# Two exp tiles of a pair turned by VectorE and moved in one set of larger transfers, with new engine orders

## Chip, cores and metric

One core of a Trainium2 chip runs the whole program in one launch. The metric is the device time of one execution in microseconds. Names used here: PE is TensorE's matmul, PEld its weight load, DVE is VectorE, ACT is ScalarE, POOL is GpSimd, SP is SyncE, whose queue issues most DMA transfers (SPq). PSUM is the memory into which PE writes.

## The reference

Attention over 2 x 8 heads (sequence 1152, width 64, queries averaged in pairs to 576), then two dense blocks on the 1152 tokens of width 512:

```python
def _attn_ref(q, k, v):
    q_pool = q.reshape(B, H, S // 2, 2, D).mean(axis=3)
    scores = scale * np.matmul(q_pool, k.transpose(0, 1, 3, 2))
    scores = scores - np.max(scores, axis=-1, keepdims=True)
    attn = np.exp(scores)
    attn = attn / (np.sum(attn, axis=-1, keepdims=True) + 1e-09)
    return np.matmul(attn, v)

def _moe_ref(x, w_in, w_out):
    h = x @ w_in
    g = np.maximum(h, 0.0) + np.log1p(np.exp(-np.abs(h)))
    return g @ w_out

def _moe2_ref(x, w_gate, w_val, w_out, rms_g):
    rms = np.sqrt(np.mean(x * x, axis=-1, keepdims=True) + 1e-06)
    xn = x / rms * rms_g
    return (silu(xn @ w_gate) * (xn @ w_val)) @ w_out
```

All inputs are float32, and the kernel keeps their precision by splitting operands into a rounded high part and a low rest (three products in place of one).

## The kernel before

The attention goes over 8 pairs of heads (`NP`, index `pb`), and in each pair over tiles `x` of 128 queries: four for each head (`NF`, tiles 0 to 3) and one mixed tile of 64 queries of both heads (`x == NF`, tile 4). One step of a tile is: scores on PE into PSUM (`qk`, L700), the row maximum on DVE (`softmax`, L714), the exps on ACT (L716) into a buffer `p`. The product with v (`av`, L778) needs the exps with keys on the partitions, so each 128x128 piece has to be turned. In most tiles PE turns them: `flip` (L735) makes 18 transposes a tile (9 blocks of keys, two heads) in five groups into PSUM, and ACT or DVE copies each group out into the buffer `pt` (`copy`, L357 and L359), five copies a tile. `flip_m` (L1188) does it for the mixed tile.

Tiles in `STREAMED`, tile 1 of pairs 1 to 6, go another way: `stream` turns the exps in blocks of 32x32 with two DVE transposes (L756, one for each head) into a buffer `turned`, and 16 DMA transfers on SP (L761) carry the blocks to their partitions in `moved`, from which `av` reads in place of `pt`. A transfer carries 32 partitions of 576 columns, 72 KB.

`prep` loads q, k and v of the next pair (L368) and makes their parts: `kk` (k with its low rest, on POOL or DVE, L362) and `qh`, `ql` (L675, L677, L617). `scales` and `shift` divide by the sums. During the attention the weights of the first dense block are decoded beside it (`decode`, called through `first_pair` and `first_out`): the weights arrive as pairs of words, L427 on ACT, L432 and L438 on DVE put them together, then a rounding copy (ACT) and a subtraction (POOL or DVE) make the halves. In the "exp" form this is done in two cuts of 512 columns; in the "soft" form, used after the attention, in one of 1024, with one more DVE operation (L435) and the subtraction on DVE. Two blocks of `w1`, and two of `w1o` (`first_out`, called in pairs 6 and 7), are decoded in the attention.

Behind it stand the two dense blocks, long runs of products (`product`, L893; `expand`, L959 to L961; `alone_in`, L980; `main_out`, L1394). The first expansion with the second block of `w1o` reads its halves at its own place in PE's order.

What sets the order of the work is a list written out in the kernel, `ORDER`: one word for each of 2314 operations, a letter for the engine (p PE, v DVE, a ACT, g POOL, s SP) and the operation's number in the source. Each engine runs its words in that order; waits between engines follow from the buffers. The marker word n1 stands where the attention's buffers are given back. `AREAS` are the columns of the memory areas, from which `alloc` cuts buffers; a buffer cut from a place used before waits for all work on the earlier one. At the start `heat` runs transposes of the identity (L1226), 20 ahead of the first scores and 16 behind the first two.

Of the kernel before, what the change touches and what calls it, by code (L numbers as in the profile page):

```python
# [37 lines left out]
AREAS = {"KF": 11264, "KR": 18432, "MR": 8704, "LR": 12800, "LF": 5120}  # L38
# [3 lines left out]
EARLY = 6.0  # L42
WAIT = 4.5
# [3 lines left out]
STREAMED = {(pb, 1) for pb in range(1, NP - 1)}  # L47
# [7 lines left out]
    p53 v7 s10 q11 v3 v8 s13 q12 a52 v6 v2 v4 v5 s14 v9 s15 v23 s16 v24 v25 s17 a35 v26 v27 s18 v36 a28 a30 v29 s19 a39 v31 a37 v40 p54 s20 v32 v38 a33 v34 s21  # L55
    v55 p57 s22 p60 v41 a56 v58 s63 a42 p91 p96 s62 v43 a92 v46 a59 p93 v47 v44 v94 a97 p98 a99 p100 v48 a95 p105 v101 p102 v45 v106 g69 p107 v103 p112 g68 a108
    p109 g70 a51 v113 s65 p114 v110 a104 s61 v71 v72 p116 a115 a111 p118 v117 p120 v119 s66 a49 p123 a86 v121 p125 a124 p127 a126 s64 v50 p130 v128 p132 a131
    a122 v87 v82 v83 p134 a133 v78 a129 p136 v135 g77 p138 g79 v137 g85 a73 s221 p141 p143 v142 p145 v139 g84 a144 s222 a88 g74 a140 p148 v146 p150 g76 v149
    a147 g75 p152 v151 a80 v89 p154 v90 a153 p158 v81 s220 a155 p156 v159 g228 p161 a157 a162 p163 g229 p165 v164 g227 a160 s224 p168 v166 p170 a245 a230 s225
    v169 a167 v201 v231 s173 p192 v246 p194 v171 a232 v193 p197 v195 g235 p199 a198 s67 g236 a196 p211 v200 g237 s172 p213 v212 g234 p215 v214 a241 g238 p218  # L60
    v216 p268 a219 g243 s223 a239 p271 v269 a217 g242 s348 v250 a270 s226 p273 g244 a272 p276 s347 v274 p278 a277 g233 p281 a275 v279 v251 a282 p283 a280 p285
    p287 v284 s266 a286 v202 s255 p290 a247 s260 p292 v288 p294 a293 s203 a291 s263 v248 a289 v240 p297 s267 p299 v295 g354 s253 a298 g353 s262 v355 s257 a296
    s258 p301 v300 v371 p303 s256 v175 a174 p307 v302 s207 a304 s259 v249 p305 p310 a306 s204 v372 a311 v308 p312 s261 p314 a313 s205 a356 s265 p317 p319 a318
    v330 s206 a309 v315 s254 s252 v357 s350 p321 a320 v176 a316 p323 v322 s351 p326 v324 a184 p328 a327 s264 s346 p337 a329 a325 p339 v338 p341 v178 g210 a340
    p344 g363 v342 p394 a345 g209 p397 g208 v395 a343 g364 v376 a396 p399 v367 a398 p402 v400 g362 p404 a403 g369 s502 p407 v405 a401 g368 p409 s503 v408 a406
    p418 v410 s349 v373 p420 a419 v331 p422 a421 v377 s332 a358 p425 p427 p429 v423 a428 s388 g361 a426 s385 g360 s380 p432 v430 a424 p434 s381 g359 s378 v433
    a431 s382 v365 s391 g370 p436 v435 a375 s336 p438 v437 p442 s392 v374 v366 a439 s334 p440 a414 s386 p445 g508 v441 g185 v443 a446 p447 s335 p449 a448 s333
    a177 s384 g509 p452 v450 p454 a453 s390 a444 s387 v510 s389 v485 a451 v415 s393 p476 s379 v179 p478 a455 s383 v477 g180 a186 p481 s352 v479 p483 a482 s501
    v181 a480 p492 v182 p496 v484 g413 v493 g187 a188 p494 v497 p499 a495 p549 s505 g412 a500 a498 g183 p552 v550 s506 g411 v532 a551 p554 v531 a553 a190 p557
    p562 a558 p559 v555 g191 a522 p564 v563 g189 a556 v560 p569 v486 a565 s543 a561 p573 s535 v526 v513 s487 p571 a570 p580 v527 v574 g516 s544 a511 s504 a572  # L70
    g524 p576 v581 p578 a577 s537 a579 p583 s536 a575 p585 v514 s507 v512 v584 a582 g517 s542 g515 p587 v586 s533 p589 a588 v523 s491 a590 v518 p591 s489 v519
    a592 p596 v528 s633 v520 p593 a597 v521 a530 v525 p598 s541 p603 v594 p600 s634 a599 a416 p605 v601 s488 a595 g417 s548 s490 v604 v616 a602 s545 v529 p607
    v640 s538 p609 v608 g639 a606 s540 g641 p612 v610 s546 p614 a613 s547 a642 s539 p623 a657 v615 a611 s534 v643 p627 s632 v624 p625 v658 v628 p630 a626 p680
    a631 g567 p683 v681 a629 g566 s637 g568 a682 s636 v662 p685 s456 a644 v684 p688 v686 p690 a689 g646 p693 v691 a687 p695 s457 g649 g648 v694 a692 g650 v663
    p702 s635 a696 a703 p704 v617 p706 a705 s665 a653 g645 s669 p709 v707 p711 s677 p713 a651 g654 s674 v712 a710 s618 a659 g655 a708 p716 v714 s671 p718 g647
# [91 lines left out]
class Plan:  # L167
# [36 lines left out]
    def around(self, tag, cols, bufs, areas, end=0):  # L204

        bases = [self.alloc(cols, areas, end) for _ in range(bufs)]
# [105 lines left out]
def body(ctx: ExitStack, tc: tile.TileContext, kT, qT, v, w1, w1o, wg, wv, w2o, rg, outM, outR):  # L312
# [651 lines left out]
    def tile_ring():  # L964
        return rings["g"]()
# [626 lines left out]
```

## Time and profile before

| what | value |
|---|---|
| time, median of 3 runs | 653.26 us (651.52 to 653.35) |
| the profiled execution: its time | 651.38 us |
| the profiled execution: its span, first to last instruction | 649.6 us |
| PE busy | 639.1 us, 98% of the span |
| DVE busy | 489.5 us, 75% |
| ACT busy | 393.4 us, 61% |
| POOL busy | 154.1 us, 24% |
| transposes of the flips (L735) | 468 |
| DVE transposes (L756) | 12 |
| transfers `turned` to `moved` (L761) | 96 |

The busy shares are averages over the span. The attention takes about the first 236 us, the dense blocks the rest. The chain of waits follows the work that ended last back from the last instruction; in a window it shows which engine's work set the time there.

### The profile page before, as it was taken

To read this page: it belongs to the slowest core of one execution; us is meant where nothing else is said; L and a number is where in the kernel's file an instruction comes from. 1 tells how busy PE (TensorE), PEld (TensorE's weight loads), DVE (VectorE), ACT (ScalarE), POOL (GpSimd) and SP (SyncE) were. 2 spreads that over 40 slices of the span, in tenths; PEclk is the share of its full clock that TensorE was granted. 3 is DMA by queue.
4 is the path that set the end of the run, shared out by engine and by line. 5 is a ranking of instruction groups with operands and counts; after the bars stand their busy time and mean duration, and the time that the engine had idled before them with its cause. 6 is when DMAs were issued, how large, how long until landed. Compare 5 with 4: busy or idle time off the path is not lost.

```text
span 649.6 us, 11166 instructions
## 1 busy us (share of the span) xinstructions
PE 639.1 (98%) x4376; PEld 545.6 (84%) x4376; DVE 489.5 (75%) x717; ACT 393.4 (61%) x647; POOL 154.1 (24%) x156
## 2 busy tenths in 40 slices
PE   7999999999999999999999999999999999999997
PEld 6888999898889988888888888888888888888886
DVE  8889889888898878887787477659898778766210
ACT  5777788788878876555553584355455544553221
POOL 0442435344523531020210033201010020104010
PEclk9999999999999999999999999999999999999999
DMA  6454544667474540332301110300542231310002
GB/s 182 125 179 104 145 102 122 155 188 189 101 202 106 159 144 1 125 135 98 126 37 66 65 66 2 129 1 0 195 147 80 99 129 66 131 65 1 34 32 81
DMA packets 25026, 66.78 MB, mean 103 GB/s; under 512 B 5327, under 2 KB 6286, under 8 KB 24974
## 3 DMA queue, kind: packets, MB, share of 16 engines
q1 hardware_dynamic: 24462, 65.68, 33.0%
q8 instruction: 34, 0.56, 0.4%
q10 hardware_dynamic: 512, 0.40, 0.2%
q14 instruction: 18, 0.15, 0.1%
HBM read 56.59 MB, written 2.39 MB: 91 GB/s over the span
## 4 chain that ended last, share of the span: by engine, by line
PE 95%; DVE 2%; ACT 1%; issue 1%; DMA 1%; ACTq 0%; DVEq 0%
PE s L893 25%; PE t L778 12%; PE s L700 12%; PE s L1394 9%; PE t L735 8%; PE t L893 4%; PE s L961 3%; PE s L959 3%; PE s L960 3%; PE t L1394 3%; PE t L980 2%; PE s L980 2%; PE t L1006 2%; PE s L1006 1%; PE t L1188 1%; PE t L961 1%
## 5 line engine op out<-in xcount | busy, mean ns | idle before, releaser
L714 DVE TENSOR_REDUCE nm<-s 128x1 f32<-128x1152 f32 x72 | 97.1, 1352 | 15.1 <-PE s L700 13.9
L716 ACT ACTIVATE p<-s,nm 128x1152 f32<-128x1152 f32 x72 | 88.1, 1225 | 14.4 <-DVE nm L714 13.6
L735 PE MATMUL t<-ident,p 128*128 128x128 f32 x468 | 69.0, 278 | 2.4 <-ACT p L716 1.3
L357 ACT COPY pt<-t 128x512 f32<-128x512 f32 (+2 forms) x105 | 54.2, 534 | 27.6 <-PE t L735 20.9
L778 PE MATMUL t<-pt,v 128*64 128x128 f32 (+1 forms) x1224 | 66.8, 263 | 0.0
L778 PEld LDWEIGHTS t<-pt,v 128*64 128x64 f32 x1224 | 59.6, 137 | 6.7 <-issue 4.5
L357 ACT CAST areaKR<-areaKF 128x1024 fp32r<-128x1024 f32 (+1 forms) x52 | 46.5, 896 | 29.6 <-PE t L1394 14.7
L735 PEld LDWEIGHTS t<-ident,p 128*128 128x128 f32 x468 | 53.0, 141 | 12.5 <-issue 3.4
L362 POOL TENSOR_TENSOR areaLR<-areaLF,areaLR 128x512 fp32r<-128x512 f32 x11 | 17.7, 1610 | 148.1 <-ACT areaLR L357 110.6
L362 DVE TENSOR_TENSOR areaKR<-areaKF,areaKR 128x1024 fp32r<-128x1024 f32 (+1 forms) x36 | 39.2, 1093 | 15.7 <-ACT areaKR L357 15.6
L893 PE MATMUL s<-areaMR,areaKR 128*128 128x512 f32 x192 | 49.0, 395 | 0.0
L362 DVE TENSOR_TENSOR areaKF<-areaKF 128x256 f32<-128x256 f32 (+1 forms) x91 | 48.0, 552 | 0.6
L893 PE MATMUL s<-areaKR 128*128 128x512 f32 x180 | 46.7, 397 | 0.0
L438 DVE SCALAR_TENSOR_TENSOR areaKF<-areaKF 128x1024 int32<-128x1024 int32 (+1 forms) x38 | 45.7, 1206 | 0.9 <-ACT areaKF L427 0.2
L357 ACT CAST areaLR<-areaKF 128x1024 fp32r<-128x1024 f32 (+1 forms) x33 | 29.2, 890 | 24.3 <-DVE areaKF L362 12.8
L362 POOL TENSOR_TENSOR kk<-kr,kk 64x384 fp32r<-64x384 f32 x35 | 34.7, 1007 | 34.3 <-ACT kk L357 26.0
L893 PEld LDWEIGHTS s<-areaMR,areaKR 128*128 128x128 f32 x192 | 35.3, 188 | 7.6
L427 ACT ACTIVATE areaKF<-areaKF 128x1024 f32<-128x1024 f32 (+1 forms) x38 | 39.9, 1054 | 1.2 <-DMA areaKF<-in_w1o_dram 1.0
L893 PEld LDWEIGHTS s<-areaKR 128*128 128x128 f32 x180 | 32.9, 188 | 6.9
L893 PE MATMUL s<-areaKR,areaLR 128*128 128x512 f32 x144 | 37.1, 396 | 0.0
L362 POOL TENSOR_TENSOR qs<-qr 128x224 f32<-128x224 f32 (+1 forms) x35 | 20.9, 617 | 66.3 <-DVE qm L636 21.2
L359 DVE COPY pt<-t 128x512 f32<-128x512 f32 (+2 forms) x49 | 30.0, 621 | 6.8 <-PE t L735 3.3
(274 smaller groups left out, 1465.7 us busy)
## 6 DMA issues: line engine op xcount, KB each, us to landing
areaKF<-in_w_dram SPq DMA_DIRECT2D x16, 512.0 KB, 5.1
areaKF<-in_w1o_dram SPq DMA_DIRECT2D x16, 512.0 KB, 4.7
qr<-in_qT_dram SPq DMA_DIRECT2D x28, 288.0 KB, 4.8
areaKF<-areaKF SPq DMA_DIRECT2D x96, 72.0 KB, 2.2
areaKF<-in_wg_dram SPq DMA_DIRECT2D x12, 512.0 KB, 4.5
areaKF<-in_wv_dram SPq DMA_DIRECT2D x12, 512.0 KB, 4.6
areaKF<-in_w2o_dram SPq DMA_DIRECT2D x12, 512.0 KB, 4.4
v<-in_v_dram SPq DMA_DIRECT2D x16, 288.0 KB, 3.4
```

The lines of the kernel that those rows point to most:

```text
L357: nc.scalar.copy(out, in_)
L359: engines[e].tensor_copy(out, in_)
L362: engines[e].tensor_tensor(out=out, in0=in0, in1=in1, op=o)
L427: o = op([act(n)], lambda e, x0=x0, x1=x1: nc.scalar.activation(out=word(1, x0, x1).bitcast(F32), in_=word(1, x0, x1).bitcast(F32), scale= ...
L438: op([dve(n)], lambda e, x0=x0, x1=x1: nc.vector.scalar_tensor_tensor(out=word(1, x0, x1), in0=word(1, x0, x1), scalar=3, in1=word(0, x0, ...
L700: nc.tensor.matmul(sc()[:, c, :N], lhsT=q()[:, cut], rhs=k()[:, c * N:(c + 1) * N], start=(i == 0), stop=(i == len(todo) - 1))
L714: u["mx"] = op([dve(S, psum=True)], lambda e: nc.vector.tensor_reduce(out=nm(), in_=sc()[:, :, :N], axis=AX.XY, op=ALU.max, negate=True), ...
L716: o = op([("ACT", 1.42)], lambda e: nc.scalar.activation(out=pr(), in_=sc()[:, :, :N], func=AF.Exp, bias=nm(), accum_out=s["den"]()[:, col ...
L735: nc.tensor.transpose(t()[:, i * P:(i + 1) * P], pr[:, c * P:(c + 1) * P], ident)
L778: nc.tensor.matmul(t()[h * D:h * D + D, :n], lhsT=s["v"][h]()[:, c, :], rhs=rhs, start=(c == 0), stop=(c == CK - 1))
L893: nc.tensor.matmul(bank(), lhsT=a(k), rhs=b(k), start=start and k + i == 0, stop=stop and k + i == 3, skip_group_check=seeded)
L1394: nc.tensor.matmul(out[m](), lhsT=w, rhs=g(), start=j + i == 0, stop=last and j == js[-1] and i == 2)
```

## The change

Tile 3 of pairs 1 to 5 is turned in the same way as tile 1 (`STREAMS`, `DOUBLE`). The two tiles of a pair share one `turned` and one `moved` of twice the size. The four DVE transposes write their parts of `turned`; the 16 transfers start when all four are done, and each carries 1152 columns, 144 KB. The products of both tiles with v run in the next pair, in the source at its tiles 2 and 3 (`WHEN`). Pair 6 still turns tile 1 alone.

The two buffers `pt` of 2304 columns become a fixed `ptwhole`, a `ptmixed` of half the size, and places inside `moved` and two later cuts (`spare`, `turned`). The areas are cut anew. The second `first_out` no longer runs in pair 7 but after the attention, in the "soft" form, in a place that the last pair's tile 3 uses until its product is done. `load` and the other transfers have new latencies in the figures with which the order was made; the kernel's run does not read them.

`ORDER` is new throughout. It has 2270 words in place of 2314. Counted in the two lists:

| words | PE | DVE | ACT | POOL | SP |
|---|---|---|---|---|---|
| before, all | 601 | 713 | 574 | 150 | 268 |
| after, all | 576 | 701 | 567 | 150 | 268 |
| before, ahead of n1 | 277 | 303 | 276 | 110 | 205 |
| after, ahead of n1 | 250 | 290 | 266 | 100 | 203 |

At the start the 16 warming transposes stand ahead of the first scores (`p53 p60 p54 p57` in place of `p53 p54 p57 p60`).

```diff
-AREAS = {"KF": 11264, "KR": 18432, "MR": 8704, "LR": 12800, "LF": 5120}
+AREAS = {"KF": 15872, "KR": 14336, "MR": 8704, "LR": 16896, "LF": 864}
+WHEN = {2: (1,), 3: (3,)}
-STREAMED = {(pb, 1) for pb in range(1, NP - 1)}
+END = NP - 2
+DOUBLE = (1, 2, 3, 4, 5)
+STREAMS = {pb: (1, 3) if pb in DOUBLE else (1,) if pb else () for pb in range(NP)} | {NP - 1: ()}
...
+    def use(self, base, first=0, n=0):
+
+        cut = slice(first * 2 * S, (first + n) * 2 * S) if n else slice(None)
+        b = Buf(lambda: base()[:, cut])
+        n = max(n, 1)
+        tail = base.__dict__.setdefault("tail", {})
+        b.area, b.prior = base.area, base.prior + [tail[x] for x in range(first, first + n) if x in tail]
+        tail.update((x, b) for x in range(first, first + n))
+        base.users.append(b)
+        self.placed.append(b)
+        return b
...
+    def place(pb, x):
+        if x == NF:
+            return places["mixed"]
+        return places["whole" if x % 2 == 0 else ("turned" if (pb, x) == (NP - 1, 3) else "spare")]
+
+    def laid_out(t, n):
+        return t().rearrange("p (b x h c j) -> p x h c b j", b=P // G, x=n, h=2, j=G)
+
     def stream(pb, x):
 
-        turned, moved = rings["turned"](), rings["moved"]()
-        units[pb, x, 0]["pt"] = moved
+        s, n = st[pb], len(STREAMS[pb])
+        i = STREAMS[pb].index(x)
+        if i == 0:
+            s["turned"], s["moved"] = plan.use(places["turned"], 0, n), plan.use(places["moved"], 0, n)
+        turned, moved = s["turned"], s["moved"]
         for h in range(2):
             pr = units[pb, x, h]["p"]
             op([("DVE", 1.37, 1)], lambda e, h=h, pr=pr: nc.vector.transpose(
-                turned().rearrange("p (b h c j) -> p h c b j", b=P // G, h=2, j=G)[:, h],
-                pr().rearrange("p k (c b j) -> p (k c) b j", b=P // G, j=G)), r=[(pr, None)], w=[(turned, h)])
+                laid_out(turned, n)[:, i, h], pr().rearrange("p k (c b j) -> p (k c) b j", b=P // G, j=G)),
+               r=[(pr, None)], w=[(turned, (i, h))])
+        if i < n - 1:
+            return
+        w = n * GW
         for b in range(P // G):
             for a in range(P // G):
                 op([("SP", 0.62)], lambda e, a=a, b=b: nc.sync.dma_start(
-                    out=moved()[b * G:(b + 1) * G, a * GW:(a + 1) * GW], in_=turned()[a * G:(a + 1) * G, b * GW:(b + 1) * GW]),
-                   r=[(turned, 0), (turned, 1)], w=[(moved, (a, b))], lat=4.0)
-
-    def av(pb, x):
+                    out=moved()[b * G:(b + 1) * G, a * w:(a + 1) * w], in_=turned()[a * G:(a + 1) * G, b * w:(b + 1) * w]),
+                   r=[(turned, None)], w=[(moved, (a, b))], lat=2.4)
+
+    def av(pb, x, more=False):
...
-    early = {(1, 0): [(first_pair, 0, HURRY[0])], (3, 0): [(first_pair, 1, HURRY[1])], (6, 0): [(first_out, 0, HURRY[2])],
-             (7, 0): [(first_out, 1, HURRY[3])]}
+    early = {(1, 0): [(first_pair, 0, HURRY[0])], (3, 0): [(first_pair, 1, HURRY[1])], (7, 0): [(first_out, 0, HURRY[2])]}
...
+            if x in STREAMS[pb]:
                 stream(pb, x)
                 qk(pb, x + 1, 0)
-                av(*prev)
-                qk(pb, x + 1, 1)
-                prev = late.pop() if late else None
-                late.append((pb, x))
+                avs(then + before)
+                if x < NF - 1:
+                    qk(pb, x + 1, 1)
+                after()
                 continue
...
     rooms(3)
+    first_out(1, "soft", FS, RS)
     first_out(2, "soft", FS, RS)
     first_pair(2, "soft", FS, RS)
```

## Rows read from the trace of the kernel before

**Rows 1.** The page's first part: busy us, share of the span, instructions.

```profile
PE 639.1 (98%) x4376; PEld 545.6 (84%) x4376; DVE 489.5 (75%) x717; ACT 393.4 (61%) x647; POOL 154.1 (24%) x156
```

**Rows 2.** The chain's shares by line: 30.96 to 231.65, then 170.15 to 199.67 us.

```profile
by line: PE s L700 34.4%; PE t L778 33.8%; PE t L735 22.9%; PE t L1188 3.4%; issue 0.9%; DVE qlB L617 0.8%; DVE kk L362 0.8%; DVE nm L714 0.7%; ACT p L716 0.7%; ACT pt L357 0.6%; DVE pt L359 0.6%; PE t L1191 0.4%; DVE O L359 0.2%; DVEq L359
...
by line: PE t L778 32.7%; PE s L700 30.3%; PE t L735 19.9%; DVE qlB L617 5.8%; DVE kk L362 5.4%; issue 2.8%; DVE pt L359 2.4%; PE t L1188 0.4%; PE t L1191 0.4%
```

**Rows 3.** Windows: length, busy us of PE, PEld, DVE, ACT, POOL, clock, DMA, GB/s.

```profile
30.96:231.65 200.69, 197.38 (x2127) 179.50 (x2126) 172.32 (x229) 163.59 (x287) 84.72 (x99) 1.00 0.55 150
142.40:170.15 27.75, 27.73 (x303) 25.30 (x302) 23.35 (x31) 24.26 (x44) 14.71 (x17) 1.00 0.53 138
170.15:199.67 29.52, 28.09 (x302) 25.40 (x302) 27.07 (x35) 23.84 (x41) 11.93 (x14) 1.00 0.59 156
```

**Rows 4.** The chain in order of time, pair from 57.60: start us, us, what.

```profile
66.45 2.12 PE t L778 x36
68.56 0.59 PE t L735 x4
69.15 1.05 PE s L700 x6
70.20 0.44 PE t L735 x4
```

**Rows 5.** Groups by line, whole span: busy us, mean ns, idle before and releasers.

```profile
L357 ACT COPY pt<-t 128x512 f32<-128x512 f32 (+2 forms) x105 | 54.2, 534 | 27.6 <-PE t L735 20.9 <-PE t L1188 3.1 <-PE t L1191 2.1
...
L359 DVE COPY pt<-t 128x512 f32<-128x512 f32 (+2 forms) x49 | 30.0, 621 | 6.8 <-PE t L735 3.3 <-PE t L1188 2.3 <-PE t L1191 0.9
...
L756 DVE STREAM_TRANSPOSE areaKF<-p 128x1152 f32<-128x1152 f32 x12 | 16.2, 1355 | 0.0
```

**Rows 6.** Transfers of L761: landing; then timeline of SP and PE, one set.

```profile
DMA to landing us min/median/max: 1.9/2.2/4.4
...
110.59 1.18 SPq L761 DMA_DIRECT2D areaKF<-areaKF  x2
...
123.61 4.39 SPq L761 DMA_DIRECT2D areaKF<-areaKF  x7
...
137.39 2.19 PE L778 MATMUL t<-areaKF,v 128*64 128x128 f32 x36
```

**Rows 7.** Timeline of DVE, then POOL, 167 to 179 us: start, us, what, idle.

```profile
167.26 1.36 DVE L756 STREAM_TRANSPOSE areaKF<-p 128x1152 f32<-128x1152 f32 x1
...
171.80 0.62 DVE L617 SCALAR_TENSOR_TENSOR qlA<-qs,qhA 128x512 fp32r<-128x512 f32 x1
...
174.33 0.29 DVE L359 COPY O<-t 128x128 f32<-128x128 f32 x1 [0.22 <-PE t L778]
...
177.96 1.69 DVE L617 SCALAR_TENSOR_TENSOR qlB<-qs,qhB 128x512 fp32r<-128x512 f32 x1
...
167.33 1.99 POOL L362 TENSOR_TENSOR kk<-kr,kk 64x384 fp32r<-64x384 f32 x2 [3.77 <-issue]
...
176.01 3.10 POOL L362 TENSOR_TENSOR areaKR<-areaKF,areaKR 128x512 fp32r<-128x512 f32 x2
```

**Rows 8.** Behind the attention: one window, then timelines of PE and DVE.

```profile
250.00:271.00 21.00, 21.00 (x105) 17.59 (x104) 18.86 (x30) 13.31 (x21) 1.63 (x1) 1.00 0.03 7
...
242.16 3.23 PE L778 MATMUL t<-pt,v 128*64 128x128 f32 x72
...
271.19 0.39 PE L959 MATMUL s<-areaLR,areaMR 128*128 128x512 f32 x1
...
250.03 0.69 DVE L432 TENSOR_SCALAR areaKF<-areaKF 128x1024 int32<-128x1024 int32 x1
...
251.72 1.25 DVE L435 SCALAR_TENSOR_TENSOR areaKF<-areaKF 128x1024 f32<-128x1024 f32 x1
...
255.67 1.22 DVE L438 SCALAR_TENSOR_TENSOR areaKF<-areaKF 128x1024 int32<-128x1024 int32 x1
```

**Rows 9.** Timeline of PE at the start.

```profile
9.90 1.91 PE L1226 MATMUL t<-ident 128*128 128x128 f32 x16
```

More of the change, by code (lines that the diff above doesn't have):

```diff
@@ L42 @@
 EARLY = 6.0
+WHEN = {2: (1,), 3: (3,)}
+SOON = {1: (1,), 2: (3,)}
 WAIT = 4.5
@@ L59 @@
[L59 to L62, printed above, removed]
@@ L204, in around @@
     def around(self, tag, cols, bufs, areas, end=0):
-        bases = [self.alloc(cols, areas, end) for _ in range(bufs)]
+        bases = [self.alloc(cols, a, end) for a in (areas if isinstance(areas, list) else [areas] * bufs)]
         count = [0]
@@ L657, in prep @@
                 round_q(h, ("m0", "m1"), 0, f, slice(0, f))
-                op([dve(S, True), act(S)], lambda e, kk=kk, hi=hi: copy(e, kk()[hi], kr()[hi]),
-                   r=[(kr, None)], w=[(kk, ("h", c)) for c in range(KB)])
+                w = [(kk, ("h", c)) for c in range(KB)]
+                if pb in CASTS:
+                    op([("POOL", 0.6)], lambda e, kk=kk, hi=hi, h=h: nc.gpsimd.dma_start(out=kk()[hi], in_=kT[n + h]),
+                       w=w, lat=6.3, hurry=8.0)
+                else:
+                    op([dve(S, True), act(S)], lambda e, kk=kk, hi=hi: copy(e, kk()[hi], kr()[hi]), r=[(kr, None)], w=w)
                 for c, cut, m in kcuts:
@@ L726, in flip @@
         if "pt" not in first:
-            first["pt"] = ring("a", "pt", [P, CK, 2, P], F32, 2)
+            first["pt"] = plan.use(places["moved"], x // 2, 1) if pb < END and x % 2 else plan.use(place(pb, x))
         pt = first["pt"]
+        laid = lambda: pt().rearrange("p (c h q) -> p c h q", h=2, q=P)
         t = tbank()
@@ L1164, in rooms @@
             free_ring("room")
-        rings["room"] = plan.around(f"room{plan.frees}", 2 * W, n, f"KF:0:{n * 2 * W}")
+        rings["room"] = plan.around(f"room{plan.frees}", 2 * W, n, [f"KF:{i * 2 * W}:{(i + 1) * 2 * W}" for i in range(n)])
     def turn(pb, x):
@@ L1267, in body @@
                 flips[1]()
-                if prev:
-                    av(*prev)
-                    if prev in STREAMED:
-                        shift(pb - 1)
-                if pb and x == 0:
-                    scales(pb - 1)
-                    if (pb - 1, 1) not in STREAMED:
-                        shift(pb - 1)
-                flips[2]()
-                if x == 1 and late:
-                    av(*late.pop())
-                    if last:
-                        free_ring("turned", "moved")
-                    shift(pb - 1)
+                avs(then + before)
+                after()
+                flips[2]()
                 flips[3]()
@@ L1441, in body @@
     norm_flip(nb)
-    late = [plan.alloc(T, "LF KF", -1) for _ in range(3)]
+    late = [plan.alloc(T, "KF LF", -1) for _ in range(3)]
     steps = {J: seven((("wg", J), ("wv", J)), X2, *banks, m2_done(J, late[1] if J == 2 else None),
```

256 lines of the change are left out of this document (144 added, 112 removed).

## The prediction

> **What bounds the kernel now.** I read the page first. PE is busy 639.1 of 649.6 us [rows 1]. Its granted clock is 1.00 in every window, so a change of clock level plays no part [rows 3, 8]. An engine that is always busy need not always be the limit, so the chain of waits comes next, window by window. In the attention, from 31 to 232 us, the chain is PE for 34.4 + 33.8 + 22.9 + 3.4 + 0.4 = 94.9%; the other 5.1% of 200.7 us, 10.2 us, is time in which PE waited for DVE or ACT [rows 2]. Those waits are not spread evenly: in the pair from 142.40 PE is busy 27.73 of 27.75 us, in the pair from 170.15 the chain is 16.4% something else, 4.8 of 29.52 us [rows 2, 3]. Behind the attention (250 to 271 us stands for it) PE is busy 21.00 of 21.00 [rows 8]. So the reader should see two stages: a long product stage where only PE work counts, and an attention stage where PE work counts plus some 10 us of waits. The engine next to the limit in the attention is DVE, 172.3 of 200.7 us (86%), with ACT at 163.6 (82%) [rows 3].
>
> **Removed from PE.** Five tiles (tile 3 of pairs 1 to 5) lose 18 transposes each. Four take 0.44 us where nothing disturbs them, 0.11 each, and 0.59 where they follow the product with v [rows 4]. Five times 18 times 0.11 is 9.9 us. One 0.59 instead of 0.44 per tile goes too: 0.15 x 5 = 0.75 us (between 0 and 1.5). The products with v themselves stay: 2.12 us for 36 matmuls on evicted tiles, and the same spacing on moved ones, whose runs of 32 columns stay as they are [rows 4, 6]. PE is the chain wherever these transposes stand, so this is worth **10.65 us**, if nothing else becomes late.
>
> **Moved between DVE and ACT.** The same five tiles lose 25 evictions out of PSUM: 0.53 us on ACT or 0.62 on DVE as means [rows 5]. They gain ten DVE transposes of 1.355 us, 13.6 us [rows 5]. The decode of the second block of `w1o` leaves the attention: there it costs DVE two shifts and two or-operations of half the width of those in [rows 8]; I estimate them at half of 0.69 and of 1.22, 1.9 us in all. The order written in the kernel tells the rest: ahead of the marker n1 DVE has 13 instructions fewer and ACT 10 fewer. Ten were added and four went with the decode, so 19 other DVE instructions go. Each costs between 0.29 (a copy 128 wide) and 0.62 us, 5.5 to 11.8 us [rows 5, 7]. DVE thus changes by 13.6 - 1.9 less 5.5 to 11.8, between -0.1 and +6.2; I take +2, nearer to the lower end, because most of the copies that can move are the wide ones. ACT falls by about 10 x 0.53 = 5.3 us. Together they have 335.9 + 2 - 5.3 = 332.6 us in some 2 x 191, 87%; before it is 335.9 in 2 x 200.7, 84% [rows 3]. The pair without a wait ran at (23.35 + 24.26) / 55.5 = 86%, the worst one at 86.2% too [rows 3]: load alone does not decide the waits up to here, but 87% lies just past what was seen. I add **+1.5 us** to the 10.2 us of waits. Its ends are -8 (a new order could be free of them, as the wait-free pair is) and +8.
>
> A rule speaks against this part. Here the PE way costs 18 x 0.11 = 1.98 us of PE and five evictions a tile; the DVE way costs 2.71 us of DVE, the engine that is next to the limit, and transfers on top [rows 4, 5]. The Trainium skill's page "VectorE: DVE Perf Modes", section "Rules for kernel authors", says to transpose a full 128x128 on TensorE when its PSUM destination is acceptable, and to keep DVE for blocks of 32x32. By the engine-time that the rule compares, the change would lose 2.71 - 1.98 = 0.73 us a tile, 3.7 us in all; by the chain it gains 10.65, since PE's time ends last. The case in which the rule wins is the first rival below.
>
> **Transfers.** The count stays at 96, 16 for each of six pairs, but those of pairs 1 to 5 carry 144 KB instead of 72. A transfer of 72 KB lands after 1.9 to 4.4 us, median 2.2 [rows 6]. For twice the bytes I bound it by the same 2.2 and by twice that, 4.4, and take 2.6, since a landing this much longer than a single issue is mostly not bytes. SP issues two in 1.18 us, 16 in 9.4 us; interleaved with loads the set now takes from 110.59 to 128.00, 17.4 us, and the product that reads it begins at 137.39, 9.4 us later [rows 6]. After the change the set cannot start before the transposes of tile 3. By PE sums (scores twice 1.05, flips 1.98, product 2.12 a tile [rows 4]) these end about 20 us into a pair of 25.6 us; 17.4 us later is 12 us into the next pair, and its tile 2, where the first reader stands in the source, runs from about 9.5 to 15.7. The cover is thus 0 to 4 us instead of 9. I cost it at nothing; if the cover is gone, the reader waits up to 5 us in each pair, minus what PE's order puts ahead of it. The loads of the next pair's q, k and v stand in the same SP queue behind these issues.
>
> **Handover to the products.** The second block of `w1o` is now decoded after the attention in its other form: on DVE 0.69 + 1.25 + 1.22 and a subtraction of the same width, which I estimate at 1.22, 4.4 us [rows 8]. Its room lies where the last pair's tile is held, so its load waits for the double product at 242.16, and the first reader stood at 271.19 [rows 8]. That leaves 29 us less 3.2 for the products, some 5 for the load (estimated at the upper landing of [rows 6]) and 7 for a decode of three such DVE steps and two of ACT: about 14 us. But DVE is busy 18.86 of 21.0 us between 250 and 271 [rows 8]; with 4.4 us more it would be full, so something there slips unless work goes to POOL, which has 10 instructions more behind n1. Bounds 0 and +4.4; I take **+0.5 us**. The start changes too: a block of 16 warming transposes, 1.91 us, stands ahead of the first scores instead of behind them [rows 9]. It costs between 0, where PE waits for its operands at that point anyway, and its own 1.9; I take 0, because the operands are still being made by DVE then.
>
> **The sum.** -9.9 - 0.75 + 1.5 + 0.5 = -8.65 us. The profiled execution took 651.38 us (span 649.6 and 1.8 around it), which gives 642.7. The three timed runs lie from 651.52 to 653.35, so the profiled one is at their low end; I round up to **643.0 us**, 638 to 646 for this case alone.
>
> **The rivals.** *DVE becomes the bound.* If the instructions that left DVE are the short ones, DVE has 172.3 + 6.2 = 178.5 us. The most that a pair reached is 27.07 of 29.52, 91.7%, and there PE waited 4.8 us [rows 2, 3]. 178.5 / 0.917 = 194.7 us: only 6.0 us saved, and with the handover's 0.5 to 4.4 the time is about **646 to 650**. For it: DVE is the engine that ends the longest waits. Against it: the pair without waits. *The waits go as well.* If the new order keeps the attention as free as the pair from 142.40, 10.65 + 8 go and the time is **630 to 638**, about 634. For it: one pair shows that PE can be fed without a gap at 84% of DVE. Against it: fuller engines. *The transfers are late*, so the change doesn't do what it says: 2 us of waiting for the moved tiles in each of five pairs gives the gain back, **651 to 653**. *Slower: preparation collides.* At 175.6 us the next pair's k and q parts were due on DVE while POOL worked: a q part whose twin took 0.62 us took 1.69 us, and PE waited 4.8 us in all around it [rows 2, 7]. Its place is the next pair's first scores; denser DVE work and later loads make it likelier. In each of five doubled pairs, one of which has it now, that is 4 x 4.8 = 19 us more, 651.4 - 10.65 + 19 = **660**. It decides for the worse from 10.65 / 5 = 2.1 us a pair. The Trainium skill's page "SBUF — State Buffer", section "SBUF: two separate sides", describes an exclusive lock between DVE and GpSimd on a shared port pair; by that rule an operation with two SBUF inputs, as this is, waits for the whole GpSimd instruction. The 1.69 us beside 3.10 us of POOL work fits that. Against this rival: the transposes that are added do not stretch beside POOL (1.36 us at 167.26 with POOL busy from 167.33) [rows 7].
>
> **How the numbers follow.** Forecast 0.60, DVE bound 0.16, waits gone 0.12, transfers late 0.05, collisions 0.07. A measurement of this kernel can tell about 0.3%, 2 us, from no change. Faster by more than that (below 651.3): 0.60 + 0.12 + 0.11 of the DVE case = 0.83. Within 0.3%: the transfer case and 0.04 of the DVE case, 0.09. Slower: 0.08, the collisions and a rest. The range is 636 to 650: outside it lie the collisions, the late transfers and the larger part of the case without waits, about 2 in 10.
>
> **What would show it.** In the profile after: 378 instead of 468 transposes in the flips' line; 22 DVE transposes at 1.36 us; a doubled pair of about 25.6 us where PE does not wait; waits of PE in the attention of about 12 us; PE at 100% behind it. If DVE stands above 92% in the doubled pairs and ends PE's waits, the first rival holds. If PE waits for the moved tiles, the transfers are late. If it waits for k and q parts in several pairs, it is the collision. A wait of PE soon after the attention for `w1o` halves would show the handover mis-sized.

## The result, and the profile of the changed kernel

The changed kernel takes 656.9 us (median of six, 654.3 to 660.1) where the kernel before takes 653.3 beside it (651.5 to 653.7). The ratio is 1.0069, 95% interval 1.0051 to 1.0086: 3.3 to 5.6 us slower. Forecast were 643.0 us, 636 to 650. Both the sign and the range were wrong. The profiled execution is the slowest of the six (660.1 us, span 658.3), so sizes are taken below from a second kernel too that differs from the changed one in a single block of TensorE and whose profile is undisturbed ("warming block back", span 653.0).

The page's busy times of the changed kernel, for [rows 1]:

```profile
PE 633.9 (96%) x4286; PEld 541.2 (82%) x4286; DVE 502.6 (76%) x705; ACT 386.7 (59%) x640; POOL 159.3 (24%) x156
```

Two windows of it, the attention and everything behind; columns as in [rows 3], the edges are the first matmul of the mixed scores of the first and of the last pair:

```profile
34.39:239.17 204.78, 190.19 (x2036) 173.05 (x2036) 178.22 (x222) 156.84 (x282) 74.67 (x84) 0.98 0.61 156
239.17:658.30 419.13, 414.26 (x2032) 341.42 (x2031) 298.28 (x432) 206.80 (x320) 76.60 (x58) 1.00 0.23 84
```

The same two windows of the kernel before, and of the changed kernel with the warming block back:

```profile
31.85:232.55 200.70, 197.39 (x2127) 179.51 (x2126) 172.37 (x229) 163.69 (x287) 84.73 (x100) 1.00 0.55 149
232.55:649.60 417.05, 413.53 (x2032) 341.39 (x2031) 289.59 (x436) 209.26 (x324) 62.07 (x44) 1.00 0.22 77
```

```profile
32.91:233.89 200.98, 187.07 (x2036) 170.32 (x2036) 178.47 (x222) 156.67 (x282) 73.55 (x84) 1.00 0.62 159
233.89:653.00 419.11, 414.29 (x2032) 341.75 (x2031) 298.41 (x432) 206.81 (x320) 76.57 (x58) 1.00 0.23 84
```

Read the third pair of lines against the second. TensorE has 197.39 - 187.07 = 10.3 us less work in the attention, as forecast. The attention is not shorter for it: 200.98 against 200.70 us. What TensorE no longer works it waits: 200.98 - 187.07 = 13.9 us not busy, against 3.3. The start is 1.06 us longer (32.91 against 31.85) and the stage behind is 2.06 us longer. 1.06 + 0.28 + 2.06 = 3.40 us, the whole difference of the spans. In the profile of the changed kernel itself the start takes 1.5 us more and the attention 3.8 us more than in this one, at a mean clock of 0.98.

What TensorE waited for in the changed kernel, over its whole span (line and what it waited for: us in all, times, longest; the 2.3 us of the first line stand at the start, at 12.5 us):

```profile
PE t L755 <- ACT p L735: 4.0, 4, 2.3
PE t L820 <- DMA areaKF<-areaKF: 4.0, 3, 1.7
PE t L820 <- ACT areaKR L372: 2.4, 1, 2.4
PE t L820 <- ACT p L735: 1.9, 1, 1.9
PE s L719 <- DVE qlB L632: 1.4, 1, 1.4
```

The second to fourth of these are one thing. In each of the five doubled pairs, the first product that reads a moved tile waits, 0.76, 1.88, 2.39, 1.53 and 1.70 us, 8.3 us in all. The view names two other releasers that were also just done; with the warming block back the same five products wait 1.09 to 1.94 us, 7.5 in all, and the releasers named at them are partly others, and in the two runs below that halve the transfers nearly all of it goes. The chain in order of time, around one of these products, tells what it waited for (start us, us, what):

```profile
154.48 1.29 DVE areaKF L792
155.77 0.17 DVE sums L845
155.94 0.40 SPq L800
...
164.03 0.59 SPq L800
164.62 0.04 issue
164.67 5.15 DMA areaKF<-areaKF
169.82 0.75 issue
170.57 2.19 PE t L820 x36
```

From the end of the last DVE transpose to the product 14.8 us pass: 8.7 for fourteen issues of SP, 5.15 for the landing of the next transfer. In [rows 6] the median landing was 2.2 us, and the product began 9.4 us after the last issue. The 5.15 us are not the rule: the chain around the products of two other pairs has 2.95 and 3.06.

```profile
77.81 2.95 DMA areaKF<-areaKF
195.51 3.06 DMA areaKF<-areaKF
```

### The profile page after: what moved, and what is told of

The parts are those of the page before. It is cut to its first block, busy times and chain, and to the rows that moved or that the text cites. A ratio compares the mean times of both kernels' runs of the same rounds, so it can differ in the third digit from the quotient of the medians.

```text
span 658.3 us, 10968 instructions
## 1 busy us (share of the span) xinstructions
PE 633.9 (96%) x4286; PEld 541.2 (82%) x4286; DVE 502.6 (76%) x705; ACT 386.7 (59%) x640; POOL 159.3 (24%) x156
## 3 DMA queue, kind: packets, MB, share of 16 engines
HBM read 56.59 MB, written 2.39 MB: 90 GB/s over the span
## 4 chain that ended last, share of the span: by engine, by line
PE 80%; DVE 7%; SPq 5%; ACT 3%; DMA 3%; issue 2%; DVEq 0%; ACTq 0%
PE s L935 24%; PE s L1452 9%; PE t L820 9%; PE s L719 7%; PE t L755 4%; PE t L935 4%; SPq L800 4%; PE t L1452 3%; PE s L1003 3%; PE s L1001 3%; PE s L1002 3%; PE t L1022 2%; PE s L1022 2%; DVE nm L733 2%; DMA areaKF<-areaKF 2%
## 5 line engine op out<-in xcount | busy, mean ns | idle before, releaser
L733 DVE TENSOR_REDUCE nm<-s 128x1 f32<-128x1152 f32 x72 | 96.7, 1349 | 13.5 <-PE s L719 12.3
L372 ACT CAST areaLR<-areaKF 128x512 fp32r<-128x512 f32 (+1 forms) x50 | 41.6, 849 | 20.7 <-DVE areaKF L377 8.9
L377 POOL TENSOR_TENSOR areaLR<-areaKF,areaLR 128x512 fp32r<-128x512 f32 (+2 forms) x13 | 17.1, 1317 | 121.6 <-ACT areaLR L372 53.9
L372 ACT CAST areaMR<-areaKF 128x512 fp32r<-128x512 f32 (+1 forms) x33 | 24.2, 733 | 37.1 <-PE t L1452 19.2
L372 ACT CAST areaKR<-areaKF 128x512 fp32r<-128x512 f32 (+2 forms) x49 | 39.3, 807 | 9.7 <-DVE areaKF L377 4.4
L820 PE MATMUL t<-areaKF,v 128*64 128x128 f32 x576 | 36.1, 281 | 8.3 <-DMA areaKF<-areaKF 4.0
L820 PEld LDWEIGHTS t<-areaKF,v 128*64 128x64 f32 x576 | 32.8, 141 | 10.6 <-issue 5.3
L372 ACT COPY ptwhole<-t 128x512 f32<-128x512 f32 (+1 forms) x58 | 30.3, 537 | 13.6 <-PE t L755 13.1
L377 POOL TENSOR_TENSOR areaLR<-areaKF,areaMR 128x512 fp32r<-128x512 f32 x11 | 15.8, 1437 | 92.7 <-ACT areaMR L372 58.8
L820 PE MATMUL t<-ptwhole,v 128*64 128x128 f32 x576 | 35.0, 275 | 0.7 <-ACT ptwhole L372 0.7
L820 PEld LDWEIGHTS t<-ptwhole,v 128*64 128x64 f32 x576 | 31.1, 137 | 4.3 <-ACT ptwhole L372 1.9
```

The lines of the kernel that those rows point to most:

```text
L372: nc.scalar.copy(out, in_)
L377: engines[e].tensor_tensor(out=out, in0=in0, in1=in1, op=o)
L733: u["mx"] = op([dve(S, psum=True)], lambda e: nc.vector.tensor_reduce(out=nm(), in_=sc()[:, :, :N], axis=AX.XY, op=ALU.max, negate=True), ...
L820: nc.tensor.matmul(t()[h * D:h * D + D, :n], lhsT=s["v"][h]()[:, c, :], rhs=rhs, start=(c == 0), stop=(c == CK - 1))
```

## The experiments

Each ratio is against the kernel before, run on the same chip, with its 95% interval. Line numbers in a fence are those of its own kernel.

**The moved product later.** Its place in TensorE's order (words of the order string):

```diff
-p381 p383 p385 p389 p387 p392 p412 p415
+p381 p385 p389 p387 p392 p412 p383 p415
```

and so in the five doubled pairs. What hangs on the product's result, and its turn among the PSUM buffers, moves with it.

> Theory (late transfers): in the changed kernel the product of old tile 1 in each of the five doubled pairs waits for its moved tile, 8.3 us in all, and TensorE's clock falls after two of these waits. Here that product stands one tile's work (about 4 us) later in TensorE's order, nothing else is changed: the five waits should shrink from 8.3 us to under 2, and the time to 648 to 650 us. Rival (load): DVE and ACT, busy 178 and 157 of the 205 us of the attention, hold the attention at its length whatever stands first on TensorE; the waits only move to tiles of exps, and the time stays at 654 to 657 us.

Measured: 665.5 us, 1.0218 (1.0195 to 1.0241). Neither theory had this. The waits of the moved product are gone, and TensorE waits more than ever, 20.0 us in the attention (210.63 - 190.60). The largest group of its waits:

```profile
PE t L776 <- ACT p L756: 12.3, 9, 2.4
```

A reading that fits, and that no further run tests: the product of 2.1 us was what TensorE did while the next exps were made. Taken from there it leaves a hole, and at its new place it is 2.1 us more in a full stretch. The run says nothing for or against the late transfers.

**Half of the transfers.**

```diff
-op([("SP", 0.62)], lambda e, a=a, b=b: nc.sync.dma_start(
+op([("SP", 0.62)], lambda e, a=a, b=b: None if n == 2 and a > 1 else nc.sync.dma_start(
```

> Leaves out 8 of the 16 transfers of each doubled pair, so that half of the turned exps are not moved. DVE's and ACT's work, the order and the bytes of each remaining transfer stay; SP issues the set in 5 us instead of 10, and the product can start some 5 us earlier. Theory (late transfers): the five waits for the moved tiles go, 648 to 650 us. Rival (load on DVE and ACT): 654 to 657 us, with PE's waits now ended by exps and evictions.

Measured: 0.9987 (0.9972 to 1.0002), 5.3 us less than the changed kernel by the two ratios (0.82% of 652). No product waits for a moved tile any more but for 0.3 us in one pair, and in the profile the attention is 6.4 us shorter than with the warming block back, at the same work of TensorE (the profiled execution is the shortest of twelve, 648.3 us where their median is 650.6):

```profile
32.34:226.93 194.59, 187.12 (x2036) 170.16 (x2036) 177.85 (x222) 156.79 (x282) 73.46 (x84) 1.00 0.52 134
```

So the late transfers cost some 5 us of the time. But even without them the kernel is no faster than before.

**Half of the bytes.**

```diff
-out=moved()[b * G:(b + 1) * G, a * w:(a + 1) * w], in_=turned()[a * G:(a + 1) * G, b * w:(b + 1) * w]
+out=moved()[b * G:(b + 1) * G, a * w:a * w + GW], in_=turned()[a * G:(a + 1) * G, b * w:b * w + GW]
```

> Leaves out half of each transfer's columns in the five doubled pairs, so that only tile 1 of the exps is moved and tile 3 isn't: still 16 transfers a set, of 72 instead of 144 KB. Issue theory: what makes the moved tile late is the time in which SP issues 16 transfers behind the second tile's transposes (10 us a set); the size of each is worth under 0.5 us a set, so the time stays at 654 to 656 us. Bytes theory: the landing of twice the bytes is late; with half of them the waits go as they did where half the transfers were left out, 650 to 651 us.

Measured: 0.9993 (0.9982 to 1.0004), 5.0 us less than the changed kernel by the ratios. The five waits are gone but for 0.3 us each in two pairs (1.55 us are new in the pair behind, whose set had 72 KB a transfer all along, with DVE named as what ended them). The attention is 3.3 us shorter than with the warming block back:

```profile
32.20:229.90 197.70, 187.44 (x2037) 170.16 (x2036) 178.09 (x222) 156.79 (x282) 74.10 (x84) 1.00 0.49 131
```

By its time the bytes theory holds, but the edit did more than the expectation says. The transfers no longer read what tile 3's transposes write, and they no longer wait for them. In the changed kernel and with the warming block back each of the five sets starts 0.02 to 0.04 us behind the end of the last transpose; here it starts 0.14 to 2.16 us ahead of it. One pair with the warming block back, then the same pair of this run (transpose, set, product; then transpose and set of this run's pair before):

```profile
120.97 1.36 DVE L806 STREAM_TRANSPOSE areaKF<-p 128x1152 f32<-128x1152 f32 x1
122.36 10.06 SPq L814 DMA_DIRECT2D areaKF<-areaKF  x16
135.69 2.19 PE L834 MATMUL t<-areaKF,v 128*64 128x128 f32 x36 [1.25 <-ACT ptwhole L386]
```

```profile
118.36 1.36 DVE L792 STREAM_TRANSPOSE areaKF<-p 128x1152 f32<-128x1152 f32 x1
119.58 10.10 SPq L800 DMA_DIRECT2D areaKF<-areaKF  x16
131.74 2.19 PE L820 MATMUL t<-areaKF,v 128*64 128x128 f32 x36
...
91.31 1.37 DVE L792 STREAM_TRANSPOSE areaKF<-p 128x1152 f32<-128x1152 f32 x1
90.52 11.70 SPq L800 DMA_DIRECT2D areaKF<-areaKF  x16
```

In the pair shown the issues end as late behind the last transpose as they did (10.0 against 10.1 us), the product begins 2.1 instead of 3.3 us behind them, and its wait of 1.25 us is gone: that is what the bytes do. The first pair is alike (13.3 us in both, 1.9 instead of 2.7, the wait 0.32 instead of 1.09). In two others the issues end 1.3 and 1.5 us earlier behind the last transpose, so there the earlier start has its part, which this run doesn't separate.

The windows show the load on the DMA engines; first five microseconds within a set of the changed kernel, then of this run (the last two columns are the busy share of the 16 DMA engines and GB/s):

```profile
161.00:166.00 5.00, 5.00 (x56) 4.53 (x55) 4.37 (x6) 4.20 (x9) 0.28 (x1) 1.00 0.92 230
```

```profile
152.00:157.00 5.00, 5.00 (x54) 4.71 (x54) 4.11 (x7) 4.17 (x9) 2.44 (x4) 1.00 0.50 119
```

Sixteen transfers of 144 KB, one each 0.63 us, are 144 / 0.63 = 229 KB a us, near the 230 GB/s that the engines moved at a busy share of 0.92. At 72 KB the same issues ask for half of that, and the median landing is 2.1 us against 2.9. That the transfers queue behind each other at the higher rate is a reading, not shown: with half of the transfers, of 144 KB each, the engines are nearly as busy within a set (0.87 at 211 GB/s from 148 to 153 us of that run) and the median landing is 3.1 us, and still no product waits, since the set ends some 5 us earlier.

```profile
areaKF<-areaKF SPq DMA_DIRECT2D x80, 144.0 KB, 2.9
```

```profile
areaKF<-areaKF SPq DMA_DIRECT2D x96, 72.0 KB, 2.1
```

**Half of the issues on GpSimd.** All work is done.

```diff
-op([("SP", 0.62)], lambda e, a=a, b=b: nc.sync.dma_start(
+q = nc.gpsimd if n == 2 and a > 1 else nc.sync
+op([("POOL" if n == 2 and a > 1 else "SP", 0.62)], lambda e, a=a, b=b, q=q: q.dma_start(
```

and the words of these 40 issues carry g in place of s.

> The 8 transfers of each doubled set that were left out in the earlier run are made again, but issued by GpSimd at the same place of the order, beside the 8 that SP issues; all the work is done. Issue theory: two queues halve the time of the set, the five waits for the moved tiles fall from 6 to 8 us to under 2, and the time is 650 to 652 us. If GpSimd's queue lands its transfers late (the earlier runs have no transfer of this kind on it), or its preparation work is held up behind the issues, the time stays at 655 to 657 us or rises to 660.

Measured: 670.9 us, 1.0287 (1.0260 to 1.0313). The first products that read a moved tile wait longer, 3.28, 3.42, 5.79, 2.50 and 0.79 us. The landing grows on both queues:

```profile
areaKF<-areaKF POOLq DMA_DIRECT2D x40, 144.0 KB, 5.1
areaKF<-areaKF SPq DMA_DIRECT2D x40, 144.0 KB, 5.0
```

GpSimd's eight issues also stand between its own preparation steps of some 1 us; in the pair from 89.4 us they go out from 98.7 to 109 us instead of within 5, and the product begins at 113.78. From SP's first issue to GpSimd's last the five sets take 8 to 11 us, where one queue took 10 to 13, so the time of the issues was not halved and the issue theory was not put to the test. Why the landing grows is not shown.

**The same with the warming block back.**

> As the run with half of the issues on GpSimd, and the 16 warming transposes back behind the first two sets of scores. If both causes add up, 1 to 1.5 us less than that run, 649 to 651 us, and by the sum of the parts it would be the first variant that beats the kernel before.

Measured: 672.0 us, 1.0318 (1.0291 to 1.0345), no better than the run above: at such waits the place of the block shows no gain.

**A set for each tile.** Two sets of 72 KB transfers, 32 issues a pair:

```diff
-if i < n - 1:
-    return
-w = n * GW
+w = GW
+ops = plan.ops
+if i < n - 1:
+    plan.ops = plan.extra
```

(the first eight of the extra transfers stand behind the first tile's transposes, the others ahead of the second set).

> Each of the two tiles of a doubled pair gets a set of 16 transfers of 72 KB of its own; the first set is issued by SP as soon as the first tile is turned, about 7 us earlier than now, the second set follows. SP issues 32 instead of 16, 10 us more a pair. Theory that the first reader is late because its tile has to wait for the second tile's transposes: the wait for the first moved tile goes (6 to 8 us), time 648 to 651 us, if the second tile's product, which stands later in the order, does not wait. Rival: SP is then full (some 28 of 28 us a pair), the second set and the next pair's loads come late, and the time is 658 to 670 us.

Measured: 684.1 us, 1.0493 (1.0475 to 1.0511); the rival, and 14 us beyond it. The median landing is 2.1 us, and the first product of a moved tile waits in only two pairs (1.33 and 0.29 us), but SP is full, and the q pieces of the next pair are issued behind 24 transfers (timeline of SP: start us, us, what):

```profile
133.40 15.79 SPq L820 DMA_DIRECT2D areaKF<-areaKF  x24
149.29 1.18 SPq L401 DMA_DIRECT2D qr<-in_qT_dram  x2
```

The window behind these issues; TensorE, ACT and GpSimd do nothing in it while the pieces land:

```profile
150.00:155.00 5.00, 0.00 (x0) 0.00 (x0) 0.33 (x2) 0.00 (x0) 0.00 (x0) 0.88 0.89 240
```

**The last transpose earlier.** In four pairs the last transpose stands ahead of the row maximum, in the first ahead of a rounding:

```diff
-v427 s342 p431 a430 s339 a432 p436 p433 v395
+v395 v427 s342 p431 a430 s339 a432 p436 p433
```

> The changed kernel, all work done; in each doubled pair the last DVE transpose stands ahead of the row maximum (in the first, of the rounding) that it stood behind, so that the set of transfers starts 0.6 to 1.9 us earlier. If only the end of the set counts, the five waits shrink by some 1.3 us each, and the time falls by 4 to 6 us, to 651 to 652.5. If DVE's row maximum, 1.3 us later, holds up the exps by as much, the waits only change their name, and the time is 655 to 658 us.

Measured: 1.0071 (1.0053 to 1.0089), as the changed kernel. The rival's time: the waits for moved tiles fall to 0.79 and 0.29 us in two pairs, and TensorE waits for exps and preparation instead (waits of TensorE):

```profile
PE t L769 <- ACT p L749: 6.0, 4, 2.3
PE s L733 <- DVE qlB L646: 2.7, 1, 2.7
PE s L733 <- ACT p L749: 2.0, 3, 0.9
```

On DVE the end of the set and the next exps are bought from each other. The exchange is not even: TensorE is 12.3 us not busy in the attention (201.94 - 189.69), 14.6 in the changed kernel's profile, and the work of 187 us in the runs at a clock of 1.00 takes 189.69 at 0.98.

```profile
32.66:234.60 201.94, 189.69 (x2036) 173.03 (x2036) 177.41 (x222) 156.66 (x282) 73.59 (x84) 0.98 0.61 158
```

**Without tile 3's transposes.** On top of the half bytes:

```diff
-op([("DVE", 1.37, 1)], lambda e, h=h, pr=pr: nc.vector.transpose(
+op([("DVE", 1.37, 1)], lambda e, h=h, pr=pr: None if i else nc.vector.transpose(
```

> As the run with half the bytes a transfer (tile 3 of the exps isn't moved), and the ten DVE transposes of tile 3 are left out too, 13.6 us of DVE. In the half-bytes run TensorE still waits some 10 us in the attention, against 3 in the kernel before, for exps, evictions and preparation. Load theory: these waits come from DVE's added transposes; without them they fall to 3 to 5 us, and the time to 645 to 647 us. Order theory: they come from the places that the new order gives to single instructions; the time stays at 650 to 652 us.

Measured: 0.9976 (0.9966 to 0.9985), 1.1 us less than with half the bytes, with intervals that overlap a little. DVE falls from 178.09 to 165.80 us in the attention, and TensorE's time not busy only from 10.3 to 9.5 us (197.05 - 187.58):

```profile
33.60:230.65 197.05, 187.58 (x2037) 170.02 (x2037) 165.80 (x212) 156.13 (x282) 73.67 (x84) 1.00 0.50 132
```

The load theory falls: most of the waits that are left do not come from DVE's added transposes. The order theory is what is left, but it stands by exclusion; which place in the order makes each wait was not tried.

**The warming block, three times.** In the changed kernel it goes back, in the kernel before it goes ahead:

```diff
-p54 v36 v40 v41 p57 v55
+p54 v36 v40 v41 p57 p60 v55
```

> The 16 warming transposes go back behind the first two sets of scores; nothing else is changed. Theory (clock at the start): they left TensorE idle between 10 and 12 us, the granted clock then reads 0.70, 0.50 and 0.95 from 12 to 18 us, and the first pair's mixed scores came 2.5 us later than before. Put back, the first mixed scores come at 31.0 to 31.5 us and the time falls by 2 to 2.5 us, to about 654.5. Rival (operands): the start waits for the late k piece and for DVE, and the clock only fills time in which TensorE would wait anyway: time as the changed kernel's, within 0.7 us.

Measured: 1.0080 (1.0050 to 1.0110), no difference that shows beside 1.0069. The expected 2 to 2.5 us are not there. The attention's waits spread these runs over 7 us, more than what is looked for.

> The kernel before with the one thing taken over from the change: the 16 warming transposes ahead of the first two sets of scores. Theory (clock at the start): the granted clock falls between 12 and 16 us, the first mixed scores come at 33 us instead of 31, and the time is 655 to 655.5 us, 2 us more than before. Rival (operands): 653 us, as before.

Measured: 1.0016 (1.0005 to 1.0027), 0.3 to 1.8 us, about half of the 2 us expected. Its profile has the attention and the rest as before (200.66 and 417.00 us), and the first mixed scores 2.4 us later, at 34.24. The windows of the start of this run, 12 to 14 and 14 to 16 us, then the same of the kernel before (the clock is the third number from the end):

```profile
12.00:14.00 2.00, 0.92 (x5) 0.92 (x6) 2.00 (x4) 1.44 (x3) 0.00 (x0) 0.65 0.34 57
14.00:16.00 2.00, 2.00 (x9) 2.00 (x9) 1.03 (x4) 1.77 (x4) 0.00 (x0) 0.50 0.89 242
```

```profile
12.00:14.00 2.00, 2.00 (x14) 1.68 (x13) 1.81 (x5) 1.67 (x3) 0.00 (x0) 1.00 0.87 224
14.00:16.00 2.00, 1.40 (x12) 1.10 (x11) 1.96 (x3) 1.73 (x5) 0.00 (x0) 1.00 0.31 71
```

0.50 is the lower level, 1.2 GHz, and 1.00 is 2.4 GHz. With the block ahead, TensorE waits 1.80 us for the first exps between the first scores and the first flips, and in this execution the clock falls. It need not: with half of the transfers TensorE does nothing from 10 to 12 us, the clock stays at 1.00, and the first mixed scores come at 32.34 us, no later than with the block back (32.91).

```profile
10.00:12.00 2.00, 0.00 (x0) 0.00 (x0) 2.00 (x2) 1.25 (x2) 0.00 (x0) 1.00 0.89 221
12.00:14.00 2.00, 1.72 (x12) 1.69 (x13) 1.63 (x5) 1.96 (x5) 0.00 (x0) 1.00 1.01 223
```

So in these profiles the place of the block costs time where the clock falls behind the gap, and not by the gap alone.

> As the run without tile 3's transposes, and the 16 warming transposes back behind the first two sets of scores. If the place of the warming block costs what it cost in the kernel before (0.3 to 1.8 us), 1 us less than that run. Rival: no difference within 0.7 us, as in the changed kernel itself.

Measured: 0.9953 (0.9940 to 0.9965), 1.5 us less than the run without tile 3's transposes. With the moved tiles in time and DVE relieved, the place of the block shows. In the profile of that run the clock falls at this place (0.50 from 12 to 14 us), in this one it does not. This is also how far the idea goes without tile 3's transfers and transposes: 3.1 us faster than before, of 10.3 us taken from TensorE.

**Two evictions first.** On top of the warming block back, in the product stage:

```diff
-v1464 v1467 v1471 p1482 v1475
+v1464 v1471 v1475 v1467 p1482
```

> The run with the warming block back, and in the product stage two evictions on DVE moved ahead of a 1.76 us step of the decode that stood before them, at the one place where TensorE waits for DVE there (0.83 us). If that wait is part of the 2.1 us by which everything behind the attention is longer than in the kernel before, the stage behind the last mixed scores falls from 419.1 to 418.3 us and the time by 0.8 us, to about 655. Rival: the step that is now later holds up the weights decoded by it, a new wait of the same size stands some microseconds further, and the stage stays at 419.1 us.

Measured: 1.0050 (1.0025 to 1.0076). The stage behind the last mixed scores takes 418.10 us, 1.0 less, and the wait of 0.83 us is gone from the list; no new one stands behind it.

```profile
233.00:651.10 418.10, 414.03 (x2032) 341.47 (x2031) 298.62 (x432) 206.79 (x320) 75.61 (x58) 1.00 0.24 84
```

By its ratio the kernel is still slower than the one before. No variant that does all the work beat it.

## Why the prediction was wrong, point by point

**What bounds the kernel.** Right: TensorE's work sets the products' stage, and the attention is that work plus waits. Wrong in the size of the waits: 10.2 us is the share of the chain that does not run over TensorE, and on such pieces of the chain TensorE mostly had other work. By [rows 3] it was not busy for 200.69 - 197.38 = 3.3 us in the whole attention, and for 29.52 - 28.09 = 1.4 us in the pair from 170.15, where 4.8 was read; the trace names two waits there, 1.10 us for a q part and 0.32 for an eviction. So there were never 8 us of waits to win, and the price of 4.8 us in the collision rival was too high. The sign of "waits of PE in the attention of about 12 us" came near the measured 13.9 by luck, since 3.3 and not 10.2 stood there before. What the prediction did not ask is how long the attention would last if TensorE were not there; that row maxima, exps, evictions and the set of transfers, each in its place, had hardly more room is what the waits suggest, and no run shows it by itself.

**Removed from PE.** Right. 378 transposes are left of 468, and the busy time in the attention fell by 10.3 us; 10.65 was forecast. The doubled pair of 25.6 us without a wait came true for the work only: the pair from 85.70 keeps TensorE busy for 25.82 us and takes 28.19, and the next two take 30.67 and 30.49.

**Moved between DVE and ACT.** The load: DVE rose from 172.4 to 178.2 us, 5.8, where +2 was taken and +6.2 was the upper bound, so the instructions that left DVE were the short ones. ACT fell by 6.9 instead of 5.3. The wait: +1.5 us was forecast. Where neither the moved tiles nor tile 3's transposes can be late (the run at 0.9953), TensorE's time not busy is 195.72 - 187.14 = 8.6 us against 3.3, 5.3 more. This term was mis-sized by nearly 4 us, and its reason was wrong as well: mostly not DVE's load. Taking 13.6 us of transposes away gave 1.1 us. The rule of the Trainium skill's page "VectorE: DVE Perf Modes", "Rules for kernel authors", comes out right in its direction here, but not by the engine time that the forecast set against the chain: the transfers behind DVE's way cost some 5 us, DVE's own time 1.1.

**Transfers.** The step that failed. They were costed at nothing, "the reader waits up to 5 us in each pair, minus what PE's order puts ahead of it" was named as the case without cover, and the cover was estimated as 0 to 4 us. Measured, there is no cover: the reader waits 0.76 to 2.39 us in each of the five pairs. The set itself was not slower than said. It was forecast to be spread over 17.4 us among loads, as in [rows 6]; the order issues it in 10.1 to 12.8 us in four pairs, straight behind the last transpose. But the reader stands earlier than said. The forecast's times put it 15 to 21 us behind the last transpose (20 us into a pair of 25.6, and 9.5 to 15.7 us into the next); in the changed kernel the product begins 14.1 to 15.6 us behind it, and would have begun 12.1 to 14.9 us behind it without its wait. The landing was put at 2.6 us by the bytes of one transfer; the median is 2.9, and the last landings that the chain shows are 2.95, 5.15 and 3.06. Worth: 5.0 to 5.3 us of the time by the two halving runs. How much of it is the time of sixteen issues, how much the landing of 144 KB and how much the wait for tile 3's transposes stays open.

**Handover.** The reader of the second block does not wait: behind the attention the trace lists no wait of TensorE before the one at 385 us. But everything behind it takes 2.06 us more, where +0.5 was forecast. 0.83 of it is that wait, behind a decode step of 1.76 us; the run with two evictions first takes it away and is 1.0 us shorter there. 0.31 is a wait for ACT further on, read in the trace alone. About 0.8 us is more busy time in the same 2032 matmuls; where it comes from stays open.

**The warming block.** Costed at 0 with bounds 0 and 1.9, "because the operands are still being made by DVE then". In the kernel before it costs 1.0 us (0.3 to 1.8), and 2.4 us in the profiled execution, in which the clock falls. The forecast had no term for that: "a change of clock level plays no part" was read from the rows of before, where the block itself filled the gap. So the cost lies within the bounds; what the reason for 0 left out is that gap.

**The sum.** With the warming block back: -10.3 from TensorE's work, +10.6 of time not busy in the attention, +2.1 behind it, +1.1 at the start, 3.5 us; the spans differ by 3.4. The forecast had +1.5 for the waits, so 9.1 of the 12 us between forecast and measurement lie there. Split by the run with half of the transfers (194.59 - 187.12 = 7.5 us not busy, a short execution), 6.4 of the 10.6 are late transfers and 4.2 other waits; by the run with half the bytes (197.70 - 187.44 = 10.3) they are 3.6 and 7.0. What makes the other waits is not shown, and neither is the 1.1 us at the start, which is there with the block at its old place too.

**The rivals.** "The transfers are late" was the right one, with a chance of 0.05 and a price of 2 us a pair. The price was near (1.65 us a pair by the waits, 1.0 by the time); the chance was far too small for a case whose price needed only the cover to be gone, and the text had put that cover at 0 to 4 us. It was also summed alone, without the other waits. "Preparation collides" did not come: one wait of 1.45 us for a q part, in one pair, and that q part took 0.67 us itself. The 22 transposes take 1356 to 1379 ns (warming block back), whatever GpSimd does. They say nothing of the lock that the Trainium skill's "SBUF — State Buffer", "SBUF: two separate sides", states for a DVE operation with two SBUF inputs, since a transpose has one. One q part, which has two, took 1.81 us at 205.61 in the changed kernel beside GpSimd's step of 1.55 us from 205.32, where the other twelve of its size behind the start took 0.62 to 0.82; that fits the page's lock, as the 1.69 us of before did. "DVE becomes the bound" is not what happened either: DVE is busy for 81 to 92% of the pairs from 85.70 to 205.99, the time lies above that rival's 646 to 650 us, and DVE's load could be taken away for 1.1 us.

## What to carry to other kernels

When a set of transfers stands between two engines, add up the whole way from the last operation that it waits for to its first reader: here 10 to 13 us of issues and a landing of some 3 to 5 us behind the last transpose. Compare that with the place of the reader in its engine's order, pair by pair, before the set is costed at nothing. A share of the chain that runs over another engine is not time in which the first one waits: take the waits from its time not busy. When work leaves a full engine, ask what that work was covering; a step may be the filler of a wait elsewhere, and the trace of before, in which nearly everything is covered, does not show these waits.

## What had not been expected of the hardware

Waits of TensorE of some 2 us can cost more than their length. After the wait of 2.39 us in the changed kernel the product that takes 2.12 us elsewhere took 3.57, with the granted clock at 0.77 and then 0.50, the level of 1.2 GHz:

```profile
138.47 3.57 PE L820 MATMUL t<-areaKF,v 128*64 128x128 f32 x36 [2.39 <-ACT areaKR L372]
```

The windows around it, 136 to 142 us (TensorE's work is the second number, the clock the third from the end):

```profile
136.00:138.00 2.00, 0.08 (x1) 0.00 (x0) 1.03 (x1) 1.89 (x4) 1.29 (x1) 1.00 1.02 242
138.00:140.00 2.00, 1.53 (x20) 1.56 (x22) 1.38 (x1) 0.45 (x1) 1.31 (x1) 0.77 0.96 279
140.00:142.00 2.00, 2.00 (x21) 1.67 (x17) 0.89 (x3) 0.00 (x0) 0.00 (x0) 0.50 0.12 39
```

It does not come every time. Of the five waits for moved tiles in this profile the clock falls behind this one alone, where the expectation of the first run says two; in the attention it falls once more, at 156 us, behind the q part's wait of 1.45 us. And one and the same kernel (two evictions first) took from 652.9 to 662.0 us, at mean clocks from 1.00 to 0.992. The kernel before, with few waits in its attention, stays within 3.2 us beside it. And transfers issued by GpSimd took no longer to land than SP's at the same time (5.1 and 5.0 us).
